# Moving small steps of a cached-attention decode kernel to GpSimd, one power for the inverse root, contiguous weights, and another order in the last batch

## The chip, the cores and the metric

The kernel runs on one core of one Trainium2 chip. The metric is the time of one execution on the device, in microseconds (us). The core has a matrix engine (PE, with its weight loads shown as PEld), a vector engine (DVE), a scalar engine (ACT), GpSimd (POOL), and a queue engine (SP) that issues the transfers; 16 transfer engines move data between HBM and the on-chip memories SBUF and PSUM. Each engine works through its own queue in order. Engines wait for one another through semaphores.

## The reference

Two layers, each an attention block with a key/value cache followed by a small MLP mixer, for 8 batch rows of one token each. Both layers use the same weights and the same caches. Cut to what matters:

```python
def attention(x, k_cache, v_cache, wq, wo):      # x: (8, 1, 448)
    q = (x @ wq).reshape(8, 1, 16, 256).transpose(0, 2, 1, 3)
    k = repeat(k_cache, 2, axis=1)               # k_cache: (8, 8, 4096, 256)
    v = repeat(v_cache, 2, axis=1)
    p = softmax(einsum("bhqd,bhkd->bhqk", q, k) * 256 ** -0.5)
    o = einsum("bhqk,bhkd->bhqd", p, v)
    return o.transpose(0, 2, 1, 3).reshape(8, 1, 4096) @ wo

def mixer(x, w1, w2, w3, w4):                    # one token: the shifted halves are zero
    x1 = x + hs                                  # hs is zero for S = 1
    return x1 + gelu(layernorm(x1) @ w3) @ w4    # w3: (448, 1792), w4: (1792, 448)

for layer in range(2):
    x = x + attention(layernorm(x), k_cache, v_cache, wq, wo)
    x = x + mixer(layernorm(x), w1, w2, w3, w4)
```

The caches are 8 x 8 x 4096 x 256 in bf16, 2 MB of K and 2 MB of V for each pair of batch row and KV head. All shifted channels of the one-token mixer come from outside the sequence, so hs is zero and w1 and w2 drop out of the computation.

## The kernel before

The work is cut into 128 jobs, called pairs: (layer, batch row, KV head). A pair loads K and V of its head, computes the scores of two query heads, a softmax, and the weighted sum of V, and adds its share of the output projection.

**Transfers and slots.** K and V go through 27 slots of 0.5 MB in SBUF. K of a pair is loaded in two runs of two slots each (lines 527 to 531), V in four single slots (544 to 549). All loads are issued on SP in one list: K of pair n comes ahead of V of pair n - 1 (lines 757 to 763). A load waits until its slot is free, that is, until PE has used the earlier content. The weights wq come first; wo, w3 and w4 follow the first pairs (384 to 392). For the heads in KEEP_HEADS (4 to 7), K of layer 0 stays in its 16 slots and layer 1 uses it again, so that those pairs of layer 1 load V only.

**Order of the pairs** (483 to 494). For each batch row b: layer 0 of b, then heads 0 to 3 of layer 1 of b - 1, then the kept heads 7 to 4 of layer 1 of b. At the very end come heads 0 to 3 of layer 1 of row 7, which load K and V.

**One pair** (from 509). DVE transposes K in SBUF (L536, eight per pair); PE computes scores into PSUM (L559); DVE takes the maximum of each partition (L566, pm) and spreads it over two columns, one for each query head (L568, pmh); GpSimd takes the maximum over all partitions (L570, gm); DVE picks the value that belongs to the partition's query head and multiplies by minus the scale (L572, nb); ACT computes the exponential with that bias and sums it (L576, p and rs); DVE transposes p (L581, pT) and spreads the sum over two columns (L583, rsh); GpSimd adds it over all partitions (L585, db); DVE takes the reciprocal (L587, rc). PE multiplies pT by V (L598); DVE transposes the result (L603, oX); four small matmuls put it together (L609); DVE scales it (L615, oT); PE adds its share of the output projection (L627, psM). Two sets of buffers alternate from pair to pair (par).

**After the last pair of a row** comes the tail (633): the residual (L645), two layer norms (norm_at, 702), w3 (L655), GELU (L662 to L674), w4 (L682), the residual again (L689, L690). In layer 0 a third norm, the query projection (L447) and expand (457) follow, which make layer 1's query; in layer 1 the row is written out (L697). A norm ends with an inverse square root: an initial guess from the bits of the number (L725, L726) and three Newton steps (L731 to L733), all on DVE.

**The planner.** Graph.schedule (145) is a list scheduler that runs while the program is built. It gives each task a start time from written durations and priorities (10 n for pair n, with small offsets), and the order that comes out is the fixed order of each engine's queue. Dependencies become semaphore waits. A list of operations given to Graph.add becomes a chain in which each step waits for the one before, on the same engine too (128 to 132).

**GpSimd's code.** Ahead of GpSimd's first affine_select (L352) the compiled program has an instruction that exchanges GpSimd's code, and ahead of its first partition_all_reduce (L570) a second one, which loads other code. They are in no line of the kernel.

Of the kernel before, what the change touches and what calls it, by code (L numbers as in the profile page):

```python
# [6 lines left out]
P = 128  # L7
B = 8
D = 448
HQ = 16  # L10
HKV = 8
SK = 4096
DH = 256
F = 1792
CP = 112
NCC = 4
# [8 lines left out]
RSQRT_MAGIC = 0x5F3759DF  # L25

NSLOT = 27
KEEP_HEADS = (4, 5, 6, 7)
TAIL_HEADS = (0, 1, 2, 3)
# [3 lines left out]
BIG = 3.0e38  # L33
# [28 lines left out]
class Res:  # L62


    def __init__(self, psum=False):
        self.prev = []
        self.writers = []
        self.readers = []
        self.psum = psum
# [10 lines left out]
    def write(self, t):  # L80
# [4 lines left out]
        for p in self.prev:  # L85
            t.deps.setdefault(p, False)
# [180 lines left out]
def bass_interleave_layers__gqa_block_cached__mixer_s_mlp__decode_kernel(  # L267
# [43 lines left out]
    rc = [sb(f"rc{i}", [P, 2], f32) for i in range(2)]  # L311
# [19 lines left out]

    kv_pool = Pool(NSLOT)
# [11 lines left out]
    def c_zero(e):  # L344
        e.memset(id4[:, :], 0.0)
        e.memset(qsel[:, :, :], 0.0)
        return e.memset(mneg[:, :], -1.0 / D)

    ops = [c_zero]
    for j in range(4):  # L350
# [11 lines left out]
        lambda e: e.tensor_scalar(cap[:, :], own[:, :], 2.0, -1.0, ALU.mult, ALU.add),  # L362
        lambda e: e.tensor_single_scalar(cap[:, :], cap[:, :], BIG, ALU.mult),
    ], 0.8, 0, reads=[res("const")], writes=[res("own")])

    def c_dve(e):
        e.memset(wo_sb[:, 32 * D:], 0.0)
# [4 lines left out]
        for i in range(4):  # L372
# [3 lines left out]
                                        res("wpad"), res("qx0"), res("qx1"), res("qx2"), res("qx3")])  # L376
# [8 lines left out]
    dma(lambda e: e.dma_start(wo_sb[:, 0:32 * D].rearrange("p (t n) -> p t n", n=D),  # L385
                              A_wo.rearrange("(t m) n -> m t n", m=P)),
# [3 lines left out]
    dma(lambda e: e.dma_start(w4_sb[:, 0:NFT * D].rearrange("p (t n) -> p t n", n=D),  # L390
                              B_w4.rearrange("(t m) n -> m t n", m=P)),
# [3 lines left out]
    def norm(tag, src, dst, bank, nb, prio, src_res, dst_res):  # L395
# [5 lines left out]
        st = sb(f"st_{tag}", [CP, 6, nb], f32)  # L401
        sti = sb(f"sti_{tag}", [CP, nb], i32)
        rL = res(f"ln_{tag}")

        def bc(ap):
# [13 lines left out]
        v, y, a = st[:, 0, :], st[:, 1, :], st[:, 2, :]  # L419
        ops = [  # L420
            lambda e: e.tensor_scalar(v, M[0:CP, 16:16 + nb], -1.0, LN_EPS, ALU.mult, ALU.add),
            lambda e: e.tensor_single_scalar(sti[:, :], v.bitcast(i32), 1, ALU.arith_shift_right),
            lambda e: e.tensor_scalar(sti[:, :], sti[:, :], -1, RSQRT_MAGIC, ALU.mult, ALU.add),
        ]
        y0 = sti[:, :].bitcast(f32)
        for it in range(3):
            yi = y0 if it == 0 else y
            ops.append(lambda e, yi=yi: e.tensor_tensor(a, yi, yi, ALU.mult))
            ops.append(lambda e: e.tensor_tensor(a, a, v, ALU.mult))
            ops.append(lambda e: e.tensor_scalar(a, a, -0.5, 1.5, ALU.mult, ALU.add))  # L430
            ops.append(lambda e, yi=yi: e.tensor_tensor(y, yi, a, ALU.mult))
        ops.append(lambda e: e.tensor_tensor(dst, xc[:, :, :], bc(y), ALU.mult))
        g.add("dve", ops, 0.18 * len(ops), prio, reads=[rM, rL], writes=[rL, dst_res])
# [23 lines left out]
    def expand(layer, b, prio):  # L457

        X = psX[1]
        rX = res("psX1", True)  # L460
# [6 lines left out]
        g.add("pe", f, 0.4, prio, reads=[res(f"q{b}"), res("const")], writes=[rX])  # L467
        for a in range(4):
# [5 lines left out]
            g.add("act" if a % 2 else "dve", cp, 0.3, prio, reads=[rX], writes=[res(f"qx{x}")])  # L474
# [7 lines left out]

    jobs = []
    for b in range(B):
        if b == 0:
            jobs += [(0, 0, h) for h in range(HKV)]
            jobs += [(0, 1, h) for h in TAIL_HEADS]
        else:
            done = TAIL_HEADS if b == 1 else ()
            jobs += [(0, b, h) for h in range(HKV) if h not in done]  # L490
            jobs += [(1, b - 1, h) for h in TAIL_HEADS]
# [408 lines left out]
```

## Time and profile before

| | |
|---|---|
| Median of 3 runs | 1246.17 us (1244.68 to 1247.53) |
| Profiled execution: its own time | 1247.13 us |
| Profiled execution: span | 1245.2 us, 41565 instructions |
| DVE busy | 806.7 us (65%), 2867 instructions |
| PE busy / PEld busy | 711.3 us (57%) / 514.7 us (41%) |
| ACT busy | 120.4 us (10%) |
| POOL busy | 99.8 us (8%), 271 instructions |
| Transfers | 483.03 MB, mean 388 GB/s |
| Mean granted PE clock | 0.62 |

The span runs from the first to the last instruction. A row of the timeline gives the start, the duration, the engine, the line, the operation, the tiles written and read with their shapes, and in brackets how long the engine had been idle and what it waited for; "issue" means that it waited for nothing that the profile shows. A row of windows gives the stretch, its length, the busy time of PE, PEld, DVE, ACT and POOL with the number of instructions, then the granted PE clock, the busy share of the transfer engines, and GB/s.

### The profile page before, as it was taken

The numbers are of one execution on the slowest core, as the hardware profiler recorded it, in microseconds if no ns is written. First come the engines' busy times: TensorE is split into PE (matmuls) and PEld (weight loads), VectorE is DVE, ScalarE is ACT, GpSimd is POOL, SyncE is SP. The second block draws the span as 40 slices with busy tenths as digits, with TensorE's granted clock in tenths as the row PEclk, the third lists the DMA queues.
The fourth block names the chain that finished last, engine by engine and source line by source line (L and its number), as shares of the span: only waits on it lengthen the run. The fifth ranks groups of instructions, "written<-read, shape, count | busy, mean of one in ns | idle before, by whom it ended". The sixth has DMA issues, their size and how long they took to land.

```text
span 1245.2 us, 41565 instructions
## 1 busy us (share of the span) xinstructions
PE 711.3 (57%) x18532; PEld 514.7 (41%) x18532; DVE 806.7 (65%) x2867; ACT 120.4 (10%) x305; POOL 99.8 (8%) x271
## 2 busy tenths in 40 slices
PE   2325566567545765457645676456754577545764
PEld 2212354355433643236523454235542365323653
DVE  5636747666767567675766667675676756767574
ACT  0100011001010111001100010100100011100110
POOL 0000001001000000000000000000100000000000
PEclk9999966556555665556655566555655556655665
DMA  9999999999999999999999999999999999999992
GB/s 303 405 351 414 406 378 414 413 407 369 402 414 408 365 412 408 412 403 373 404 414 404 398 378 394 413 412 404 367 407 414 402 360 414 402 414 407 363 395 92
DMA packets 109667, 483.03 MB, mean 388 GB/s; under 512 B 13264, under 2 KB 19152, under 8 KB 84688
## 3 DMA queue, kind: packets, MB, share of 16 engines
q1 hardware_dynamic: 108464, 480.37, 97.3%
q8 instruction: 145, 2.38, 0.8%
q14 instruction: 34, 0.28, 0.1%
q10 hardware_dynamic: 1024, 0.01, 0.0%
HBM read 480.32 MB, written 0.01 MB: 386 GB/s over the span
## 4 chain that ended last, share of the span: by engine, by line
DMA 56%; PE 23%; DVE 13%; issue 5%; SPq 2%; ACT 1%; POOL 0%; ACTq 0%
DMA kv<-in_A_v_cache_dram 39%; DMA kv<-in_A_k_cache_dram 15%; PE psO L598 8%; DVE kv L536 6%; PE psS L559 6%; PE psX L682 3%; PE psX L447 2%; DMA wo_sb<-in_A_wo_dram 2%; PE psM L627 2%; SPq L547 1%; DVE oX L603 1%; PE psX L655 1%; SPq L530 1%; DVE pT L581 1%; PE psX L713 1%
## 5 line engine op out<-in xcount | busy, mean ns | idle before, releaser
L536 DVE STREAM_TRANSPOSE kv<-kv 128x512 int32<-128x512 int32 x768 | 506.6, 691 | 84.9 <-DMA kv<-in_A_k_cache_dram 84.9
L598 PE MATMUL psO<-kv,pT 128*2 128x256 bf16 x4096 | 268.5, 393 | 153.5 <-DMA kv<-in_A_v_cache_dram 104.5
L559 PE MATMUL psS<-kv,qx 128*8 128x128 bf16 x8192 | 253.2, 294 | 144.2 <-DVE rc L587 65.3
L559 PEld LDWEIGHTS psS<-kv,qx 128*8 128x8 bf16 x8192 | 205.8, 117 | 173.7 <-DVE rc L587 67.1
L576 ACT ACTIVATE p<-psS,nb 128x256 bf16<-128x256 f32 x128 | 107.1, 836 | 910.1 <-DVE nb L572 867.0
L598 PEld LDWEIGHTS psO<-kv,pT 128*2 128x2 bf16 x4096 | 83.6, 94 | 256.5 <-DMA kv<-in_A_v_cache_dram 184.1
L627 PE MATMUL psM<-oT,wo_sb 128*128 128x1 bf16 x2048 | 87.0, 172 | 70.8 <-DVE oT L615 60.4
L566 DVE TENSOR_REDUCE pm<-psS 128x1 f32<-128x256 f32 x128 | 53.6, 418 | 107.3 <-PE psS L559 105.8
L603 DVE STREAM_TRANSPOSE oX<-psO 128x256 f32<-128x256 f32 x128 | 57.5, 449 | 85.8 <-PE psO L598 85.6
L627 PEld LDWEIGHTS psM<-oT,wo_sb 128*128 128x128 bf16 x2048 | 76.9, 117 | 84.7 <-DVE oT L615 68.2
L570 POOL PARTITION_ALL_REDUCE gm<-pmh x128 | 46.5, 363 | 748.4 <-DVE pmh L568 582.9
L585 POOL PARTITION_ALL_REDUCE db<-rsh x128 | 51.5, 402 | 362.9 <-DVE rsh L583 326.5
L609 PE MATMUL psO<-oX,id 128*32 128x4 f32 x1024 | 37.0, 200 | 50.4 <-DVE oX L603 22.9
L609 PEld LDWEIGHTS psO<-oX,id 128*32 128x32 f32 x1024 | 29.5, 141 | 80.4 <-DVE oX L603 45.2
L581 DVE STREAM_TRANSPOSE pT<-p 128x256 bf16<-128x256 bf16 x128 | 54.1, 423 | 5.1 <-ACT p L576 3.2
L682 PE MATMUL psX<-hT,w_sb 128*128 128x1 bf16 x896 | 32.5, 171 | 19.5 <-issue 11.9
L682 PEld LDWEIGHTS psX<-hT,w_sb 128*128 128x128 bf16 x896 | 30.9, 116 | 20.7 <-issue 12.3
L655 PE MATMUL psX<-n,w_sb 112*128 112x1 bf16 x896 | 26.1, 165 | 19.6 <-DVE n L734 19.6
L447 PE MATMUL psX<-n,wq_sb 112*128 112x1 bf16 x1024 | 29.0, 165 | 14.1 <-DVE n L734 13.1
L447 PEld LDWEIGHTS psX<-n,wq_sb 112*128 112x128 bf16 x1024 | 28.0, 104 | 14.2 <-DVE n L734 13.7
L576 ACT ACTIVATION_READ_ACCUMULATOR p<-psS,nb 128x1 f32 x128 | 33.6, 262 | 0.0
L655 PEld LDWEIGHTS psX<-n,w_sb 112*128 112x128 bf16 x896 | 25.0, 103 | 20.4 <-DVE n L734 20.4
(148 smaller groups left out, 380.6 us busy)
## 6 DMA issues: line engine op xcount, KB each, us to landing
kv<-in_A_v_cache_dram SPq DMA_DIRECT2D x512, 512.0 KB, 12.9
kv<-in_A_k_cache_dram SPq DMA_DIRECT2D x192, 1024.0 KB, 16.5
wq_sb<-in_A_wq_dram SPq DMA_DIRECT2D x1, 3584.0 KB, 17.5
wo_sb<-in_A_wo_dram SPq DMA_DIRECT2D x1, 3584.0 KB, 28.3
w_sb<-in_B_w_dram SPq DMA_DIRECT2D x2, 1568.0 KB, 25.8
out_dram<-xT ACTq DMA_DIRECT2D x8, 0.9 KB, 6.5
xT<-in_A_x_dram SPq DMA_DIRECT2D x1, 7.0 KB, 2.0
```

Of the source, the lines that this page charges most:

```text
L447: last = e.matmul(M[:, base + col * nb:base + (col + 1) * nb], wq_sb[:, k, f0:f0 + P], xn[:, :, k], start=(k == 0), stop=(k == NCC - 1))
L536: return e.transpose(ap, ap)
L559: last = e.matmul(S[32 * j:32 * j + 8, w * y:w * y + w], qx[x][:, h, 2 * c + u, :], kt[:, :, c, 8 * j:8 * j + 8, u], start=(c == 0 and u = ...
L566: g.add("dve", lambda e: e.tensor_reduce(pm[par][:, :], S[:, 0:256], axis=AX.X, op=ALU.max), 0.4, pr, reads=[rS], writes=[res(f"pm{par}")])
L576: g.add("act", lambda e: e.activation(p_sb[par][:, :].rearrange("p (z k y) -> p y z k", z=8, k=8), S[:, 0:256].rearrange("p (y z k) -> p y ...
L581: g.add("dve", lambda e: e.transpose(pT[par][:, :], p_sb[par][:, :]), 0.44, pr, reads=[rP], writes=[rPT])
L598: last = e.matmul(O[32 * j:32 * j + 2, 0:DH], pt[:, i, 2 * a:2 * a + 2], slot_ap(vin)[:, i * DH:(i + 1) * DH], start=(a == 0 and i < 4), s ...
L603: g.add("dve", lambda e: e.transpose(oX[par][:, :], O[:, 0:DH]), 0.4, pr, reads=[rO], writes=[res(f"oX{par}")])
L609: last = e.matmul(O[32 * a:32 * a + 32, 256:260], id4[:, :], oX[par][:, :].rearrange("p (c a r) -> p a c r", c=2, a=4)[:, a, :, 0:2], star ...
L627: last = e.matmul(psM[layer][:, c:c + 1], wo_sb[:, c0:c0 + 509:4], oT[:, jb, kt_:kt_ + 1], start=(first and k == 0 and c == 0), stop=False ...
L655: last = e.matmul(M[:, 32 + ft:33 + ft], w3_sb[:, c, ft * P:(ft + 1) * P], xa["n2"][:, 0, c:c + 1], start=(c == 0), stop=(c == NCC - 1))
L682: last = e.matmul(M[:, 64 + c:65 + c], w4_sb[:, c0:c0 + 509:4], hT[:, ft:ft + 1], start=(ft == 0), stop=(ft == NFT - 1))
```

## The change

- KEEP_HEADS and TAIL_HEADS become KEEP_RUNS, how many of a head's two K runs stay (2 for heads 4 to 7, as before). In the last row, layer 1's heads 0 to 3 come ahead of the kept heads.
- Every norm takes the inverse root as one operation on GpSimd, a power of -0.5 (against a tile pw filled with -0.5), between two DVE steps.
- pmh, nb and rsh move from DVE to GpSimd. nb, which was one DVE instruction with an accumulator, becomes a product and a sum. pmh adds a mask of 0 and -1e38 instead of taking a minimum.
- wo is loaded so that a partition holds four neighbouring rows of a head's 512, w4 so that a partition holds 14 neighbouring rows. oX, the four small matmuls and w3's columns are rearranged to fit. A partition then belongs to one query head, so rc has one column, made on GpSimd by a product with a mask (half) and a sum, and oT is a scaling by a per-partition scalar. rc's buffers order their writes against the reads on the same engine (strict).
- The four copies of expand are tracked one by one, so DVE's and ACT's no longer take turns.
- Some written durations of the planner differ.

```diff
-KEEP_HEADS = (4, 5, 6, 7)
-TAIL_HEADS = (0, 1, 2, 3)
+KEEP_RUNS = {4: 2, 5: 2, 6: 2, 7: 2}
-BIG = 3.0e38
+BIG = 1.0e38
...
         for p in self.prev:
+            if self.strict:
+                t.deps[p] = True
             t.deps.setdefault(p, False)
...
-        lambda e: e.tensor_scalar(cap[:, :], own[:, :], 2.0, -1.0, ALU.mult, ALU.add),
-        lambda e: e.tensor_single_scalar(cap[:, :], cap[:, :], BIG, ALU.mult),
+        lambda e: e.tensor_scalar(cap[:, :], own[:, :], -1.0, BIG, ALU.add, ALU.mult),
...
-    dma(lambda e: e.dma_start(wo_sb[:, 0:32 * D].rearrange("p (t n) -> p t n", n=D),
-                              A_wo.rearrange("(t m) n -> m t n", m=P)),
+    dma(lambda e: e.dma_start(wo_sb[:, 0:32 * D].rearrange("p (h f) -> p h f", h=HKV),
+                              A_wo.rearrange("(h m k) n -> m h (k n)", m=P, k=4)),
...
-    dma(lambda e: e.dma_start(w4_sb[:, 0:NFT * D].rearrange("p (t n) -> p t n", n=D),
-                              B_w4.rearrange("(t m) n -> m t n", m=P)),
+    dma(lambda e: e.dma_start(w4_sb[:, 0:NFT * D], B_w4.rearrange("(m t) n -> m (t n)", m=P)),
...
-        rX = res("psX1", True)
+        rX = [res(f"psX1_{a}", True) for a in range(4)]
...
         else:
-            done = TAIL_HEADS if b == 1 else ()
-            jobs += [(0, b, h) for h in range(HKV) if h not in done]
-            jobs += [(1, b - 1, h) for h in TAIL_HEADS]
-        jobs += [(1, b, h) for h in reversed(KEEP_HEADS)]
-    jobs += [(1, B - 1, h) for h in TAIL_HEADS]
+            jobs += [(0, b, h) for h in range(HKV) if b > 1 or h in KEEP_RUNS]
+            jobs += [(1, b - 1, h) for h in tail_heads]
+        if b == B - 1:
+            jobs += [(1, b, h) for h in tail_heads]
+        jobs += [(1, b, h) for h in keep_heads]
...
-        g.add("dve", lambda e: e.tensor_scalar(pm2[par][:, :], cap[:, :], pm[par][:, 0:1], None, ALU.min), 0.18, pr,
+        g.add("pool", lambda e: e.tensor_scalar(pm2[par][:, :], cap[:, :], pm[par][:, 0:1], None, ALU.add), 0.25, pr,
               reads=[res(f"pm{par}"), res("own")], writes=[res(f"pmh{par}")])
         g.add("pool", lambda e: e.partition_all_reduce(gm[par][:, :], pm2[par][:, :], P, ReduceOp.max), 0.45, pr,
               reads=[res(f"pmh{par}")], writes=[res(f"gm{par}")])
-        g.add("dve", lambda e: e.tensor_tensor_reduce(
-            out=nbx[par][:, :], in0=gm[par][:, :], in1=ownneg[:, :], scale=1.0, scalar=0.0,
-            op0=ALU.mult, op1=ALU.add, accum_out=nb_[par][:, 0:1]), 0.25, pr,
-            reads=[res(f"gm{par}"), res("own")], writes=[res(f"nb{par}")])
+        g.add("pool", [
+            lambda e: e.tensor_tensor(nbx[par][:, :], gm[par][:, :], ownneg[:, :], ALU.mult),
+            lambda e: e.tensor_tensor(nb_[par][:, :], nbx[par][:, 0:1], nbx[par][:, 1:2], ALU.add),
+        ], 0.5, pr, reads=[res(f"gm{par}"), res("own")], writes=[res(f"nb{par}")])
...
-        g.add("dve", lambda e: e.tensor_scalar(rs2[par][:, :], own[:, :], rs[par][:, 0:1], None, ALU.mult), 0.18, pr + 1,
+        g.add("pool", lambda e: e.tensor_scalar(rs2[par][:, :], own[:, :], rs[par][:, 0:1], None, ALU.mult), 0.25, pr + 1,
               reads=[res(f"rs{par}"), res("own")], writes=[res(f"rsh{par}")])
-        g.add("pool", lambda e: e.partition_all_reduce(db[par][:, :], rs2[par][:, :], P, ReduceOp.add), 0.5, pr,
+        g.add("pool", lambda e: e.partition_all_reduce(db[par][:, :], rs2[par][:, :], P, ReduceOp.add), 0.45, pr + 1,
               reads=[res(f"rsh{par}")], writes=[res(f"db{par}")])
-        g.add("dve", lambda e: e.reciprocal(rc[par][:, :], db[par][:, :]), 0.17, pr + 1,
-              reads=[res(f"db{par}")], writes=[res(f"rc{par}")])
+        g.add("pool", [
+            lambda e: e.tensor_tensor(dbx[par][:, :], db[par][:, :], half[:, :], ALU.mult),
+            lambda e: e.tensor_tensor(db1[par][:, :], dbx[par][:, 0:1], dbx[par][:, 1:2], ALU.add),
+        ], 0.5, pr + 1, reads=[res(f"db{par}"), res("half")], writes=[res(f"dh{par}")])
+        g.add("dve", lambda e: e.reciprocal(rc[par][:, :], db1[par][:, :]), 0.17, pr + 1,
+              reads=[res(f"dh{par}")], writes=[res(f"rc{par}")])
...
-        g.add("dve", lambda e: e.transpose(oX[par][:, :], O[:, 0:DH]), 0.4, pr,
+        g.add("dve", lambda e: e.transpose(oX[par][:, :].rearrange("p (c r) -> p c r", r=32),
+                                        O[:, 0:DH].rearrange("p (a r k) -> p a k r", a=2, k=4)), 0.4, pr,
...
-        g.add("dve", lambda e: e.tensor_tensor(
-            oT[:, jb, 4 * h:4 * h + 4].rearrange("p (j c) -> p c j", c=2),
-            O[:, 256:260].rearrange("p (c j) -> p c j", j=2),
-            rc[par][:, :].unsqueeze(1).to_broadcast([P, 2, 2]), ALU.mult), 0.2, pr,
+        g.add("dve", lambda e: e.tensor_scalar(
+            oT[:, jb, 4 * h:4 * h + 4], O[:, 256:260], rc[par][:, 0:1], None, ALU.mult), 0.2, pr,
...
-                    last = e.matmul(M[:, 32 + ft:33 + ft], w3_sb[:, c, ft * P:(ft + 1) * P], xa["n2"][:, 0, c:c + 1],
+                    last = e.matmul(M[:, 32 + ft:33 + ft], w3_sb[:, c, ft:ft + 127 * NFT + 1:NFT], xa["n2"][:, 0, c:c + 1],
...
-        for it in range(3):
-            yi = y0 if it == 0 else y
-            ops.append(lambda e, yi=yi: e.scalar_tensor_tensor(a, yi, v, yi, ALU.mult, ALU.mult))
-            ops.append(lambda e: e.tensor_scalar(a, a, -0.5, 1.5, ALU.mult, ALU.add))
-            ops.append(lambda e, yi=yi: e.tensor_tensor(y, yi, a, ALU.mult))
-        ops.append(lambda e: e.tensor_scalar(dst, xc[:, :, :], y, None, ALU.mult))
-        g.add("dve", ops, 0.18 * len(ops), prio, reads=[rM, rL], writes=[rL, dst_res])
+        v, y = st[:, 0:1], st[:, 1:2]
+        g.add("dve", lambda e: e.tensor_scalar(v, M[0:CP, 16:17], -1.0, LN_EPS, ALU.mult, ALU.add), 0.18, prio,
+              reads=[rM], writes=[rL])
+        g.add("pool", lambda e: e.tensor_tensor(y, v, pw[0:CP, 0:1], ALU.pow), 0.6, prio,
+              reads=[rL, res("const")], writes=[rL])
+        g.add("dve", lambda e: e.tensor_scalar(dst, xc[:, :, :], y, None, ALU.mult), 0.25, prio,
+              reads=[rL], writes=[rL, dst_res])
```

## The prediction

> **What bounds the kernel now.** I read the page's slices and shares first, then the windows, then the timelines of the end and of GpSimd (POOL). On the page, "DMA" is the busy share of the 16 transfer engines and "GB/s" what they moved:
>
> ```profile
> POOL 0000001001000000000000000000100000000000
> DMA  9999999999999999999999999999999999999992
> GB/s 303 405 351 414 406 378 414 413 407 369 402 414 408 365 412 408 412 403 373 404 414 404 398 378 394 413 412 404 367 407 414 402 360 414 402 414 407 363 395 92
> ```
>
> The transfers bound the kernel: at about 411 GB/s, 483.03 MB take 1175 us of the 1245.2. The rest is a slow start, a dip once per batch, and an end without transfers. POOL is idle 92% of the time. A dip, in windows (the last two columns are DMA share and GB/s), and what ends it:
>
> ```profile
> 1160.00:1165.00 5.00, 3.30 (x113) 3.22 (x114) 1.87 (x12) 0.00 (x0) 0.00 (x0) 0.50 1.03 409
> 1165.00:1170.00 5.00, 3.71 (x101) 3.35 (x102) 2.48 (x14) 0.52 (x2) 0.00 (x0) 0.50 0.74 293
> 1170.00:1175.00 5.00, 4.19 (x150) 3.35 (x138) 3.03 (x19) 0.84 (x2) 1.11 (x3) 0.68 0.75 240
> ...
> 1168.57 3.37 PE L559 MATMUL psS<-kv,qx 128*8 128x128 bf16 x119 [0.17 <-ACT qx L473]
> ```
>
> Layer 1's scores wait for its query, so slots stay full. The dip costs 5 x (116 + 169)/409 = 3.5 us; the same sum over the eight dips (from 175, 280, 425, 575, 720, 870, 1020 and 1165 us) gives 25.4 us.
>
> One pair's small steps, unloaded, at the end of the run (columns: start, duration):
>
> ```profile
> 1219.38 0.42 DVE L566 TENSOR_REDUCE pm<-psS 128x1 f32<-128x256 f32 x1 [0.40 <-PE psO L609]
> ...
> 1219.84 0.23 DVE L568 TENSOR_SCALAR pmh<-cap,pm 128x2 f32<-128x2 f32 x1
> ...
> 1220.16 0.36 POOL L570 PARTITION_ALL_REDUCE gm<-pmh  x1 [3.10 <-DVE pmh L568]
> 1220.55 0.16 DVE L572 CUSTOM_DVE_ANT_0 nbx<-gm,ownneg 128x2 f32<-128x2 f32 x1 [0.48 <-POOL gm L570]
> 1220.64 0.08 DVE L572 DVE_READ_ACCUMULATOR2_ANT nb<- 128x1 f32 x1
> 1220.82 0.83 ACT L576 ACTIVATE p<-psS,nb 128x256 bf16<-128x256 f32 x1 [4.96 <-DVE nb L572]
> ```
>
> Finally POOL's first instructions. Each row ends with its idle time before and the releaser:
>
> ```profile
> 1.24 0.19 POOL L347 MEMSET mneg<- 112x112 f32 x1
> 11.99 0.32 POOL L352 TENSOR_SCALAR_AFFINE_SELECT qsel<-qsel 128x128 bf16<-128x128 bf16 x1 [10.56 <-issue]
> ...
> 14.14 0.21 POOL L355 TENSOR_SCALAR_AFFINE_SELECT id<-id 128x32 f32<-128x32 f32 x1
> 32.96 0.38 POOL L570 PARTITION_ALL_REDUCE gm<-pmh  x1 [18.61 <-DVE pmh L568]
> ```
>
> This is what decides my forecast. POOL stands 10.56 us ahead of its first AFFINE_SELECT and waits for nothing that the profile shows. In the compiled program an instruction that exchanges GpSimd's code stands there, and a second, for other code, stands ahead of the first PARTITION_ALL_REDUCE, where 18.61 us of idle time would hide it. MEMSET ran before either. So one set of code serves AFFINE_SELECT and another the all-reduce, and an exchange costs up to 10.56 us. Before pays for two, because after the constants POOL runs only all-reduces (256).
>
> **The change, part by part.**
>
> *Small steps to POOL.* Per pair this takes pmh (203 ns), nbx with its accumulator read (141 + 83) and rsh (196) off DVE: 26.0 + 18.1 + 10.7 + 25.0 = 79.8 us of DVE's 806.7, beside the transfers. It puts on POOL one TENSOR_SCALAR and two TENSOR_TENSOR around each of the two all-reduces. No POOL row shows these. One costs between 0.10 (MEMSET 128x1) and 0.40 us (all-reduce); I take 0.21, the 128x32 AFFINE_SELECT, the nearest in kind. POOL's chain for a pair, without exchanges: six steps x 0.21 = 1.26, all-reduces 0.36 + 0.40, the exponential in between 0.1 + 0.82 + 0.1 (1220.82 to 1221.64 with its accumulator read), and six waits on its own results x 0.1 (the all-reduce starts 0.09 after pmh ends) = 0.6: together 3.6 us.
>
> Whose code do the new steps need? If they are resident as MEMSET is, no exchange. If they share the all-reduce's code, one at the start. If they need AFFINE_SELECT's or other code, the order "scale, all-reduce, multiply, add; scale, all-reduce, multiply, add" changes code four times per pair, in a queue that runs in order. I take four: the profile's own name for the instruction that asked for the first set is TENSOR_SCALAR_AFFINE_SELECT, so the tensor-scalar family is the nearest row, and it is not in the all-reduce's set.
>
> Price of an exchange, from rows: above, 10.56 us, seen while the transfer engines were 0.85 to 1.06 busy; below, 1.28 us, ScalarE's ACT_TABLE_LOAD, the only other load of this kind that shows. With the transfer engines idle I take midway, 5.92; beside the stream, 10.56. In a run of some 4200 us the stream needs 1175, a share of 0.28: 0.28 x 10.56 + 0.72 x 5.92 = 7.22 us. A pair then holds POOL for 4 x 7.22 + 3.6 = 32.5 us, against 9.5 us of transfers. 128 x 32.5 = 4160 us. Nothing overlaps it: each exchange lies between two steps of one chain, and the next pair's steps queue behind it on POOL; the exponential waits for them, then pT, PV, the slots and SP's transfers.
>
> The Trainium skill, GPSIMD Engine Reference, section Instruction dispatch, says that GpSimd's kernels are loadable code and that the first call after a load pays about 6 us (5.95 measured), with no instruction visible in the profile. Put in for the 7.22, that gives 128 x (4 x 5.95 + 3.6) + 82 = 3590 us, an estimate. Its section Engine selection speaks against the change outright: elementwise work belongs on VectorE.
>
> *Inverse root.* In the end's norm the chain runs from 1228.05 to DVE's last step at 1230.53: 2.48 us. It becomes one DVE step (0.17), a hop (0.09), the power and a hop back (0.03). The power lies between 0.10 and 0.40 us by POOL's rows; at 0.40, the dearer, it saves 1.8 us. Two norms lie on the end's path: 3.6. The other 38 and the prologue's go beside POOL's chain. A power needs no exchange where it falls among the other new steps. In layer 0's tail, the Newton steps queue between K transposes (0.69 us each) for 7.9, 8.1 and 2.7 us (1126.59 to 1134.53, 1138.62 to 1146.69, 1159.37 to 1162.11). Without them the query comes some 15 us sooner, which would close the dips if transfers still set the pace. POOL may wait for powers and queries: 0 to 48 us over 16 tails (3 each); I take 30.
>
> *wo and w4.* The page's "under 2 KB" minus "under 512 B" is 5888 pieces, which is 4096 + 1792 of 896 B: exactly wo and w4. They become 1024 pieces of 3584 B and 128 of 12.5 KB. Between 52 and 76 us the stream lost 5.4 us. V's 4 KB pieces run at 411 GB/s, so 0 to 5.4 is gained; I take 4.8, hidden when POOL sets the pace. w3's weights are then read at a stride of 14: between L655's 1.66 and L682's (stride 4) 1.97 us for 56 matmuls, so 0 to 0.3 us per tail.
>
> *Order of the last batch.* K's transposes (about 5.2 us per pair) leave the last four pairs; oX came every 8.8 and 7.0 us there, a V-only pair needs 5.1 us of transfers. With the hole at 1207 to 1209 (1.4) this is 0 to 3.2 us, hidden in the POOL case, too. On SP's queue 8 K and 16 V transfers move ahead of 16 V transfers; kept K then holds 16 of the 27 slots for four pairs more. Batch 6's four pairs ran like that at 385 to 421 GB/s (1120 to 1140 us), so that costs at most 5 x (411 - 385)/411 = 0.3 us in a window.
>
> *The rest.* Two copies of the query run side by side (about 0.8 us per expansion); oX, the four small matmuls, oT and rc keep their sizes (within 0.05 us each); the four memsets of half lie in DVE's idle 4.3 to 14.4. The new planner durations reorder the queues; no row prices that, and I allow 10 us either way (a third of what dips and weights lose together).
>
> *Sum* against the profiled execution (1247.13 = span 1245.2 + 1.9; 0.96 above the median of 1246.17): start to the first all-reduce 33.0, pairs 4160, waits 30, end 20.1 (1225.06 to 1245.2) - 3.6 = 16.5: span 4240, **4240 us** with the 1.9.
>
> **Rivals.**
> - *No exchanges (faster).* The steps are resident as MEMSET is: POOL needs 3.6 us per pair, far below 9.5. Then three quarters of the dips (19; PE, at 3.3 to 4.2 of 5 us there, keeps some) go, with 4.8 of the weights and about 5 of the end: 1247 - 29 = 1218 us. For it: MEMSET ran freely. Against: AFFINE_SELECT didn't. It also decides if exchanges are cheap: 4 x s + 3.6 stays below 9.5 while s is under 1.5 us, as at the lower row's 1.28.
> - *Two exchanges per pair.* If half of the changes fall away (neighbouring all-reduces, or one kind shared): 128 x (2 x 7.22 + 3.6) + 82 = 2390 us. The fixed chain of a pair speaks against it.
> - *Exchanges always at full price*, if loading doesn't get faster without the stream: 128 x (4 x 10.56 + 3.6) + 82 = 5950 us. It is the forecast's upper end; at 5.92 each the forecast is 3574.
>
> **How the numbers follow.** Four exchanges per pair: 0.86, with 0.06 of it near full price. Two: 0.03. None or cheap: 0.11, of which 0.01 lands within 0.2%, about what a measurement of this kernel can tell from no change. So faster 0.10, same 0.01, slower 0.89. The range leaves out the rivals on the near side and a little more, and goes from 3300 (an exchange of 5.4 us) to 6000.
>
> **What would show it.** Right: POOL rows with idle times of 5 to 11 us "<-issue" ahead of each all-reduce and of the step after it, some 500 of them; DMA share near 0.3; the chain of waits mostly issue or POOL. Wrong: a POOL TENSOR_TENSOR within 0.3 us of its all-reduce; then the dips, the 52 to 76 us stretch and the Newton rows tell how much of the 29 us came.

## The result, and the profile after

The changed kernel takes 4695.7 us (median of 4 runs, 4679.3 to 4711.3) where the kernel before takes 1245.4 us beside it: 3.770 times as long, with a 95% interval of 3.756 to 3.784. The profiled execution took 4711.25 us, with a span of 4709.3.

The slices of the page after, where the transfers stood at 411 GB/s before, and the shares of the chain that ended last:

```profile
DMA  8113412332123321233212332123321233213230
GB/s 295 72 72 121 152 50 112 125 112 87 66 112 125 112 84 68 112 125 112 81 72 111 126 112 81 68 113 127 112 81 69 113 128 112 82 62 116 108 116 1
issue 81%; DVE 7%; POOL 6%; PE 3%; ACT 2%; POOLq 1%; DMA 0%; ACTq 0%; SPq 0%
```

The transfers are no longer the bound. 81% of the chain is "issue", time in which an engine waits for nothing that the profile shows. GpSimd's waits (engine, line and what ended the wait; then us in total, times, longest) say where:

```profile
POOL gm L574 <- issue: 1035.9, 128, 11.5
POOL dbx L592 <- issue: 941.9, 121, 12.2
POOL nbx L577 <- issue: 844.6, 114, 12.0
POOL db L589 <- issue: 809.9, 127, 9.0
POOL pmh L572 <- DVE pm L570: 420.4, 104, 22.7
POOL rsh L587 <- ACT p L580: 131.8, 126, 1.3
```

Ahead of each all-reduce (gm, db) and of the first step behind it (nbx, dbx) stands a wait of 6 to 8 us on average: four per pair. In the compiled program 511 instructions exchange GpSimd's code, for 2 before. The trace fits them: behind the first AFFINE_SELECT, GpSimd's queue goes 510 times from an all-reduce to an elementwise step or back, and each of these 510 steps has waited for "issue", 5.7 us or more. The fifth row is a different wait, for the next pair's maximum (its longest, 22.65 us, stands ahead of the very first pair, which leaves 398 us between the pairs). One pair and the start of the next, in the timeline of the kernel after (start, duration; in brackets the idle time before, and the releaser):

```profile
2054.99 0.41 POOL L589 PARTITION_ALL_REDUCE db<-rsh  x1 [6.64 <-issue]
2063.00 0.19 POOL L592 TENSOR_TENSOR dbx<-db,half 128x2 f32<-128x2 f32 x1 [7.60 <-issue]
2063.26 0.19 POOL L593 TENSOR_TENSOR db<-dbx 128x1 f32<-128x1 f32 x1
2063.49 0.16 DVE L595 RECIPROCAL rc<-db 128x1 f32<-128x1 f32 x1 [14.64 <-POOL db L593]
...
2065.43 1.07 PE L563 MATMUL psS<-kv,qx 128*8 128x128 bf16 x32
...
2067.48 0.42 DVE L570 TENSOR_REDUCE pm<-psS 128x1 f32<-128x256 f32 x1 [0.62 <-PE psS L563]
...
2068.02 0.31 POOL L572 TENSOR_SCALAR pmh<-cap,pm 128x2 f32<-128x2 f32 x1 [4.56 <-DVE pm L570]
...
2079.30 0.37 POOL L574 PARTITION_ALL_REDUCE gm<-pmh  x1 [10.98 <-issue]
```

Two steps of the same kind follow each other at once (dbx, then db at 2063.26); a change of kind costs 6.64, 7.60 and 10.98 us here. The row of 2063.49 shows the second loss: DVE, which works in order, has stood for 14.64 us at the reciprocal of the old pair, and only behind it come the work that lets PE make the next pair's scores (here the copies of layer 1's query, in most pairs the transposes of K, for which PE waits 1720.2 us in all), and their maximum. GpSimd, which has just got its elementwise code back, waits 4.56 us more for that maximum.

A pair takes (4689.5 - 31.2)/128 = 36.4 us, from the first pair's first step on GpSimd to the last pair's last. The sum of the four "issue" rows, with the smaller ones of the same kind (51.8 ahead of db's second step, 58.4 and 43.6 ahead of 14 powers), is 3786 us: 29.6 per pair, 7.40 each.

### The profile page after: what moved, and what is told of

It is laid out like the page before. It is cut to its first block, busy times and chain, and to the rows that moved or that the text cites. A ratio compares the mean times of both kernels' runs of the same rounds, so it can differ in the third digit from the quotient of the medians.

```text
span 4709.3 us, 42358 instructions
## 1 busy us (share of the span) xinstructions
PE 754.1 (16%) x18532; PEld 557.9 (12%) x18532; DVE 729.1 (15%) x1904; ACT 119.5 (3%) x305; POOL 300.5 (6%) x1081
## 4 chain that ended last, share of the span: by engine, by line
issue 81%; DVE 7%; POOL 6%; PE 3%; ACT 2%; POOLq 1%; DMA 0%; ACTq 0%; SPq 0%
DVE kv L540 5%; ACT p L580 2%; PE psS L563 2%; POOL db L589 1%; POOL gm L574 1%; DVE pm L570 1%; POOL rsh L587 1%; POOL pmh L572 1%; POOL nb L578 1%; POOL db L593 1%; POOL dbx L592 1%; POOL nbx L577 1%; DMA kv<-in_A_k_cache_dram 0%; DVE rc L595 0%; POOLq L592 0%
## 5 line engine op out<-in xcount | busy, mean ns | idle before, releaser
L563 PE MATMUL psS<-kv,qx 128*8 128x128 bf16 x8192 | 257.5, 301 | 2220.8 <-DVE kv L540 1720.2
L540 DVE STREAM_TRANSPOSE kv<-kv 128x512 int32<-128x512 int32 x768 | 492.3, 681 | 20.6 <-DMA kv<-in_A_k_cache_dram 20.5
L563 PEld LDWEIGHTS psS<-kv,qx 128*8 128x8 bf16 x8192 | 192.2, 115 | 2280.8 <-DVE kv L540 1764.0
L595 DVE RECIPROCAL rc<-db 128x1 f32<-128x1 f32 x128 | 21.0, 164 | 1818.3 <-POOL db L593 1818.3
L606 PEld LDWEIGHTS psO<-kv,pT 128*2 128x2 bf16 x4096 | 116.5, 115 | 578.2 <-issue 541.0
L662 PE MATMUL psX<-n,w_sb 112*128 112x1 bf16 x896 | 56.4, 198 | 226.3 <-DVE n L733 226.3
L592 POOL TENSOR_TENSOR dbx<-db,half 128x2 f32<-128x2 f32 x128 | 23.6, 185 | 941.9 <-issue 941.9
L662 PEld LDWEIGHTS psX<-n,w_sb 112*128 112x128 bf16 x896 | 55.1, 160 | 230.1 <-DVE n L733 230.1
L577 POOL TENSOR_TENSOR nbx<-gm,ownneg 128x2 f32<-128x2 f32 x128 | 23.6, 184 | 844.6 <-issue 844.6
L572 POOL TENSOR_SCALAR pmh<-cap,pm 128x2 f32<-128x2 f32 x128 | 38.9, 304 | 422.8 <-DVE pm L570 420.4
L587 POOL TENSOR_SCALAR rsh<-own,rs 128x2 f32<-128x2 f32 x128 | 38.8, 303 | 131.8 <-ACT p L580 131.8
```

The lines of the kernel that those rows point to most:

```text
L540: return e.transpose(ap, ap)
L563: last = e.matmul(S[32 * j:32 * j + 8, w * y:w * y + w], qx[x][:, h, 2 * c + u, :], kt[:, :, c, 8 * j:8 * j + 8, u], start=(c == 0 and u = ...
L572: g.add("pool", lambda e: e.tensor_scalar(pm2[par][:, :], cap[:, :], pm[par][:, 0:1], None, ALU.add), 0.25, pr, reads=[res(f"pm{par}"), re ...
L577: lambda e: e.tensor_tensor(nbx[par][:, :], gm[par][:, :], ownneg[:, :], ALU.mult),
L587: g.add("pool", lambda e: e.tensor_scalar(rs2[par][:, :], own[:, :], rs[par][:, 0:1], None, ALU.mult), 0.25, pr + 1, reads=[res(f"rs{par}" ...
L606: last = e.matmul(O[32 * j:32 * j + 2, 0:DH], pt[:, i, 2 * a:2 * a + 2], slot_ap(vin)[:, i * DH:(i + 1) * DH], start=(a == 0 and i < 4), s ...
```

## Experiments

Two theories were set against each other first. Theory 1: GpSimd exchanges its code whenever its queue changes between an all-reduce and an elementwise step. Theory 2: the price hangs on the moved small steps themselves, and not on what they alternate with. Later runs ask where the sum went wrong, and what the other parts of the change are worth.

| Run | What it is | Time (us) | Ratio to before, 95% | Exchanges in the program |
|---|---|---|---|---|
| after | the whole change | 4695.7 | 3.756 to 3.784 | 511 |
| e1 | after, small steps and Newton on DVE | 1258.3 | 1.0126 to 1.0176 | 2 |
| e2 | after, all-reduces replaced | 1226.3 | 0.9855 to 0.9902 | 1 |
| e3 | e1 with rsh alone on GpSimd | 2767.5 | 2.222 to 2.236 | 258 |
| e4 | after, small steps on DVE | 1381.3 | 1.1103 to 1.1152 | 51 |
| e5 | after, planner's durations corrected | 4156.1 | 3.333 to 3.354 | 509 |
| e6 | before, small steps on GpSimd | 4090.7 | 3.280 to 3.302 | 510 |
| e7 | e1 with the order of before | 1247.3 | 1.0006 to 1.0044 | 2 |
| e8 | e7 with w3 and w4 as before | 1241.6 | 0.9974 to 1.0011 | 2 |
| e9 | after, dbx and db on DVE | 4047.2 | 3.250 to 3.273 | 501 |
| e10 | e8, inverse root on ScalarE | 1225.1 | 0.9852 to 0.9891 | 2 |
| e11 | e8, two Newton iterations | 1229.0 | 0.9882 to 0.9929 | 2 |
| e12 | e10 and e11 together | 1223.9 | 0.9848 to 0.9887 | 2 |

### Is it the change of code?

**e4: the small steps back on DVE, the powers left on GpSimd.**

```diff
-        g.add("pool", lambda e: e.tensor_scalar(pm2[par][:, :], cap[:, :], pm[par][:, 0:1], None, ALU.add), 0.25, pr,
+        g.add("dve", lambda e: e.tensor_scalar(pm2[par][:, :], cap[:, :], pm[par][:, 0:1], None, ALU.add), 0.18, pr,
```

(likewise nbx and nb, rsh, dbx and db)

> As e1, but the inverse root is the power on POOL: 51 exchanges, those around the powers of the 16 tails. Theory 1 (alternation): each exchange runs beside the full stream and takes 8 to 11.5 us, as the dearest of the changed kernel did; two of them ahead of a pair's all-reduce are more than the 13 us that 11 free slots buffer, so about half a tail's 18 us or more is lost in most of the 16 tails: 1290 to 1400 us. Theory 2 (the steps themselves): 41 powers of 0.6 us, hidden, and the shorter norms close the dips: 1200 to 1225 us.

1381.3 us, as theory 1 had it and 156 us above the upper end of theory 2. The waits of e4's GpSimd for "issue" name the cause, a power between two all-reduces:

```profile
POOL gm L574 <- issue: 119.5, 15, 11.4
POOL st_0c L731 <- issue: 86.3, 8, 11.9
POOL st_1a L731 <- issue: 84.5, 8, 12.3
POOL st_0a L731 <- issue: 77.7, 8, 11.6
```

Against e1, which differs in the power alone, that is 123 us: the inverse root as one power is itself a loss of 10% while the all-reduces stand on the same engine. An exchange costs 9.7 to 10.8 us ahead of these powers (86.3/8, 84.5/8, 77.7/8), beside a stream above 380 GB/s in most of them, and 8.0 back (119.5/15).

**e2: no all-reduce at all.** Each of the two becomes an elementwise GpSimd instruction that copies the partition's own value, so the maximum and the sum over the partitions are left out.

```diff
-e.partition_all_reduce(gm[par][:, :], pm2[par][:, :], P, ReduceOp.max)
+e.tensor_scalar(gm[par][:, :], pm2[par][:, :], one1[:, 0:1], None, ALU.mult)
-e.partition_all_reduce(db[par][:, :], rs2[par][:, :], P, ReduceOp.add)
+e.tensor_scalar(db[par][:, :], rs2[par][:, :], one1[:, 0:1], None, ALU.add)
```

> The changed kernel with both all-reduces replaced by one more elementwise TENSOR_SCALAR on POOL each, so that POOL never changes its code after the start. It leaves out the maximum and the sum over the partitions; everything else, all the new POOL steps and the power among them, stays. Theory 1 (alternation): 1200 to 1235 us, POOL rows follow one another without idle time of several us that nothing explains. Theory 2 (the steps themselves): above 4000 us, since POOL has two steps more of the new kind. Theory 3 (order, layout, planner): near 4700.

1226.3 us with all eight elementwise steps of a pair on GpSimd. The steps follow one another at once; the longer waits are for other engines:

```profile
607.25 0.29 POOL L574 TENSOR_SCALAR pmh<-cap,pm 128x2 f32<-128x2 f32 x1 [5.05 <-DVE pm L572]
607.63 0.29 POOL L576 TENSOR_SCALAR gm<-pmh,one 128x2 f32<-128x2 f32 x1
608.01 0.19 POOL L579 TENSOR_TENSOR nbx<-gm,ownneg 128x2 f32<-128x2 f32 x1
```

Theory 2 falls: the same steps cost nothing where nothing alternates with them.

**e3: one step of the pair on GpSimd** (rsh), Newton and the other steps on DVE, so that neighbouring all-reduces of two pairs have nothing between them.

```diff
 # e1, and:
-        g.add("dve", lambda e: e.tensor_scalar(rs2[par][:, :], own[:, :], rs[par][:, 0:1], None, ALU.mult), 0.18, pr + 1,
+        g.add("pool", lambda e: e.tensor_scalar(rs2[par][:, :], own[:, :], rs[par][:, 0:1], None, ALU.mult), 0.25, pr + 1,
```

> As e1, but of the six small steps one, rsh (the spreading of the sums, TENSOR_SCALAR 128x2), stays on POOL between the two all-reduces: 258 exchanges in the compiled program instead of 511 or 2. Theory 1 (alternation): two exchanges of about 7.4 us per pair, of which the first overlaps the exponential (1.3 us), plus some 3 us of chain: 16 to 19 us per pair, 2050 to 2500 us; idle time of 5 to 11 us ahead of rsh and ahead of the second all-reduce, and none ahead of the first. Theory 2 (each new step costs its share): a sixth of the loss of 3450 us, about 1820 us.

Two exchanges per pair, as theory 1 says, but 2767 us, above its range. A pair of e3 in the timeline:

```profile
1399.75 0.29 POOL L597 TENSOR_SCALAR rsh<-own,rs 128x2 f32<-128x2 f32 x1 [9.34 <-issue]
1405.92 0.41 POOL L599 PARTITION_ALL_REDUCE db<-rsh  x1 [5.88 <-issue]
...
1411.21 0.37 POOL L584 PARTITION_ALL_REDUCE gm<-pmh  x1 [4.88 <-DVE pmh L582]
...
1419.95 0.29 POOL L597 TENSOR_SCALAR rsh<-own,rs 128x2 f32<-128x2 f32 x1 [8.37 <-issue]
```

The exchanges took 8.8 (1126.5/128) and 6.8 us (823.7/121), 15.6 of a pair's 21.2 ((2745.9 - 33.5)/128, from the first all-reduce to the last). Nearly 5 us more pass between the two all-reduces in these rows, for the next pair's K transposes, scores and maximum on DVE and PE, which stand behind the denominator. My range had no term for that; it is the same gap as in the forecast.

**e6: the small steps alone, on the kernel before.**

```diff
 # before, and only:
-        g.add("dve", lambda e: e.tensor_scalar(pm2[par][:, :], cap[:, :], pm[par][:, 0:1], None, ALU.min), 0.18, pr,
+        g.add("pool", lambda e: e.tensor_scalar(pm2[par][:, :], cap[:, :], pm[par][:, 0:1], None, ALU.add), 0.25, pr,
```

(likewise nbx and nb, and rsh; pmh's mask changes with it; the denominator has no sum in this layout)

> The kernel before with the small steps of a pair alone moved to GpSimd: 510 exchanges; norms, weights, order and durations otherwise as before. If the small steps alone are the cause: 510 exchanges of 7.4 us (3774 us), 300 us of GpSimd's own work and a wait of the kind seen ahead of pmh, so 4400 to 4800 us, within 5% of the changed kernel. If another part of the change were needed for the slow-down (the power between the steps, the new order): under 3000 us.

4090.7 us: the small steps alone make 2845 us of the slow-down, but the 4400 to 4800 was missed from below. 510 exchanges, one fewer than after, and 605 us less time: the changed kernel loses something else, too.

### What the other 605 us are

**e9: the denominator's product and sum back on DVE**, as one instruction that reads the all-reduce.

```diff
-        g.add("pool", [
-            lambda e: e.tensor_tensor(dbx[par][:, :], db[par][:, :], half[:, :], ALU.mult),
-            lambda e: e.tensor_tensor(db1[par][:, :], dbx[par][:, 0:1], dbx[par][:, 1:2], ALU.add),
-        ], 0.5, pr + 1, reads=[res(f"db{par}"), res("half")], writes=[res(f"dh{par}")])
+        g.add("dve", lambda e: e.tensor_tensor_reduce(
+            out=dbx[par][:, :], in0=db[par][:, :], in1=half[:, :], scale=1.0, scalar=0.0,
+            op0=ALU.mult, op1=ALU.add, accum_out=db1[par][:, 0:1]), 0.25, pr + 1,
+            reads=[res(f"db{par}"), res("half")], writes=[res(f"dh{par}")])
```

> The changed kernel with one of its steps undone: the denominator's product and sum (dbx, db) are again one DVE instruction that reads the all-reduce's result; 501 exchanges stay. Theory A (what the changed kernel takes over e6's 4091 us comes from that step alone: on GpSimd it stands behind an exchange, DVE's reciprocal waits for it, and the next pair's maximum stands behind the reciprocal, so one of the four exchanges and the next pair's preparation come one after the other): the reciprocal follows the all-reduce directly, the exchange back runs beside the next pair's preparation, the pmh wait for DVE's pm falls from 420 to under 120 us: 4050 to 4200 us. Theory B (the new order, the powers on GpSimd or the durations make the difference): 4550 to 4720 us.

4047.2 us, theory A and 3 us beyond its range. Ten exchanges fewer explain 74 us; the span fell by 664. The same place in e9's timeline:

```profile
2080.10 0.41 POOL L589 PARTITION_ALL_REDUCE db<-rsh  x1 [6.00 <-issue]
2080.54 0.16 DVE L591 CUSTOM_DVE_ANT_0 dbx<-db,half 128x2 f32<-128x2 f32 x1 [6.37 <-POOL db L589]
...
2084.90 0.42 DVE L570 TENSOR_REDUCE pm<-psS 128x1 f32<-128x256 f32 x1 [1.13 <-PE psS L563]
...
2087.21 0.29 POOL L572 TENSOR_SCALAR pmh<-cap,pm 128x2 f32<-128x2 f32 x1 [6.70 <-DVE kv L540]
```

DVE goes on 0.03 us after the all-reduce, and the next pair's maximum is done at 2085.32, while the exchange back is still running (to 2087.21). In the kernel after, DVE went on only after that exchange, so the two came one behind the other. Most of it can be read in the waits: exchanges and pmh's waits together are 3786 + 420 = 4206 after, and here 857.7 (gm) + 817.3 (db) + 907.2 (nbx) + 861 (pmh, whatever ended it) + 183 (powers) = 3626, 580 of the 664; the two steps that left GpSimd, 0.45 us a pair (2063.00 to 2063.45 above), are 58 more. (pmh's wait has a new name here, since the last semaphore to come was DVE's, but the exchange is inside it.)

**e5: only the planner's durations corrected.**

```diff
-e.partition_all_reduce(gm[par][:, :], pm2[par][:, :], P, ReduceOp.max), 0.45, pr,
+e.partition_all_reduce(gm[par][:, :], pm2[par][:, :], P, ReduceOp.max), 7.8, pr,
```

(likewise the other all-reduce; 8.2 for the two steps behind each)

> The changed kernel with only the planner's durations corrected: 7.8 us for an all-reduce and 8.2 us for the two steps behind it, which is what they cost with their exchanges in the profile after. It still has 509 exchanges. Theory A (the 420.4 us for which GpSimd waits ahead of pmh come from DVE's queue, which was laid out for steps of 0.45 us and so stands at the reciprocal while the next pair's scores and maximum are behind it): the planner now puts the next pair's work ahead of that reciprocal, the wait falls to under 100 us, and the time to 4300 to 4400 us. Theory B (the wait lies in the chain of one pair itself, whatever the order): the wait stays near 420 us and the time within 50 us of 4696.

4156.1 us: theory A, and more than it asked for. Of the waits for DVE's maximum one is left, 22.4 us ahead of the first pair, and gm's exchange is cheaper, 746.3/126 = 5.9 us where it was 8.1:

```profile
POOL db L589 <- issue: 826.3, 127, 8.6
POOL gm L574 <- issue: 746.3, 126, 7.9
POOL rsh L587 <- issue: 638.3, 64, 12.8
POOL pmh L572 <- issue: 506.0, 58, 14.8
```

Others are dearer in return, 638.3/64 = 10.0 us ahead of rsh and 506.0/58 = 8.7 ahead of pmh, so that all of e5's exchanges together take 3631 us, 155 less than after. The rest of the gain is the wait for the maximum.

The price of an exchange goes with the stream beside it. Three windows, of after, e5 and e9, each the time of one exchange ahead of gm (last two columns: DMA share and GB/s):

```profile
2068.00:2079.30 11.30, 1.89 (x74) 1.49 (x72) 1.15 (x6) 0.00 (x0) 0.31 (x1) 0.62 1.01 398
```

```profile
2033.40:2039.30 5.90, 4.25 (x120) 3.48 (x120) 1.32 (x3) 0.83 (x2) 0.00 (x0) 0.55 0.01 4
```

```profile
2087.60:2096.80 9.20, 0.00 (x0) 0.00 (x0) 0.61 (x2) 0.00 (x0) 0.00 (x0) 0.50 0.62 257
```

10.98 us at 398 GB/s, 5.94 at 4, 9.30 at 257. Over all 255 exchanges to the all-reduce's code in the kernel after, the 74 with under 20 GB/s beside them took 5.99 us on average, and the 15 with over 380 took 10.0, but single ones from 6.4 to 11.5: the rate alone doesn't fix the price. In after the pair's new transfers go out just when gm's exchange begins; in e5's window it runs with the stream at rest.

### What the other parts are worth

**e1: all of the change but the steps and the power** (pieces as in e4, and before's Newton steps).

> The changed kernel with the six small steps of a pair and the inverse root (Newton steps) back on DVE; contiguous weights, the new order of the last batch, the split copies and the planner durations stay. POOL then runs only the all-reduces after the constants, so the compiled program exchanges GpSimd's code twice instead of 511 times. Theory 1 (the alternation between the all-reduce's code and the elementwise code costs the time): 1205 to 1240 us, about 5 us from the weights and up to 5 at the end below the 1245 of before. Theory 2 (the new steps themselves are slow on POOL): the same, 1205 to 1240. Theory 3 (the new order, the new layout or the planner durations cost the time): far above 1300.

1258.3 us: not faster but 1.3 to 1.8% slower than before. Something else in the change costs more than it brings. e1's windows show a hole at the new order of the last batch:

```profile
1160.00:1165.00 5.00, 0.68 (x16) 0.59 (x16) 4.64 (x19) 0.00 (x0) 0.00 (x0) 0.50 0.98 399
1165.00:1170.00 5.00, 3.51 (x128) 3.49 (x128) 1.44 (x6) 0.00 (x0) 0.00 (x0) 0.50 0.07 29
1170.00:1175.00 5.00, 4.01 (x119) 3.81 (x120) 3.50 (x20) 0.52 (x2) 0.06 (x1) 0.50 0.19 23
```

Before ran at 293 and 240 GB/s in the last two. SP's queue stands for 14.3 us for layer 1's scores, which wait for their query (the longest such wait of before in this stretch: 10.3).

**e7: e1 with before's order of the last batch.**

```diff
-        if b == B - 1:
-            jobs += [(1, b, h) for h in tail_heads]
         jobs += [(1, b, h) for h in keep_heads]
+    jobs += [(1, B - 1, h) for h in tail_heads]
```

> e1 (all of the change but the steps and the power on GpSimd) with the last batch in the order of before. e1 took 1258.3 us, 13 to 16 more than before. If the new order is why: its stream stood at 29 and 23 GB/s from 1165 to 1175 us, which is 5 x (382 + 388)/411 = 9.4 us lost, where before lost 3.5 there; 5.9 us come back: 1250 to 1254. If the order is innocent: 1256 to 1261, and the cause is the weights read at a stride or the planner's durations.

1247.3 us: 11.0 less than e1 (nearer 16 by the two ratios to before, 1.0151 and 1.0025), twice or more what the hole at 1165 us explained. A second one of e1, at 1200 to 1210 us (215 and 342 GB/s), would be worth 5 x (196 + 69)/411 = 3.2 us; 2 us, or 7 by the ratios, stay open. The new order is a loss.

**e8: w3 and w4 as before, too.**

```diff
-w3_sb[:, c, ft:ft + 127 * NFT + 1:NFT]
+w3_sb[:, c, ft * P:(ft + 1) * P]
```

(and w4's load as before, in pieces of 896 B)

> e7 with w3 and w4 laid out as before too (w3's weight loads contiguous, w4 in pieces of 896 B), so that wo alone is contiguous. If the stride of 14 costs what the changed kernel's end shows (3.52 for 1.66 us, 1.9 per tail, one of them on the end's path and the others ahead of a query): 2 to 6 us under e7, so 1246 to 1251 by the order theory. If the small pieces of w4 cost more than the stride: above e7 by up to 2 us.

1241.6 us, under the range and 5.7 below e7 (their intervals just overlap). The weight loads of w3 in e7's layout, shown by e1, and in e8's (mean ns of one ahead of the bar that gives the idle time):

```profile
L672 PEld LDWEIGHTS psX<-n,w_sb 112*128 112x128 bf16 x896 | 55.3, 160 | 30.5 <-DVE n L751 25.0 <-issue 2.3 <-DVE kv L550 1.9
```

```profile
L672 PEld LDWEIGHTS psX<-n,w_sb 112*128 112x128 bf16 x896 | 25.2, 104 | 32.4 <-DVE n L751 24.5 <-issue 4.3 <-DVE pT L595 2.0
```

A column stride of 14 makes a weight load 160 ns for 104, so each tail's 56 take 3.5 us for 1.7. What is left of the change in e8 (contiguous wo, the copies side by side, the layout of oX, other planner durations) can't be told from no change.

**e10: the inverse root on ScalarE.** e8, with every tail norm but the last tail's as a logarithm and an exponential.

```diff
+        g.add("act", lambda e: e.activation(v, M[0:CP, 16:17], ACT.Ln, bias=eps1[0:CP, 0:1], scale=-1.0), 1.5, prio,
+              reads=[rM, res("const")], writes=[rL])
+        g.add("act", lambda e: e.activation(y, v, ACT.Exp, scale=-0.5), 1.5, prio, reads=[rL], writes=[rL])
+        g.add("dve", lambda e: e.tensor_scalar(dst, xc[:, :, :], y, None, ALU.mult), 0.25, prio,
+              reads=[rL], writes=[rL, dst_res])
```

> e8 with the inverse root of all tail norms but the last tail's as two ScalarE steps, a logarithm and an exponential, in place of the eleven DVE steps. 76 table loads of about 1.28 us (97 us) come with it, on an engine that is 10% busy. If DVE's queue is what makes the dips (the Newton steps between K transposes): the query of layer 1 comes 5 to 8 us sooner and the dips go as in e2, which lost 29.9 us of transfers up to 1205 us for 44.4 of before: 12 to 16 us under e8, 1225 to 1231. If the norm's hops are not on the dips' path: 1238 to 1244. If the loads hold up the exponentials of the pairs: above e8.

1225.1 us, 1.1 to 1.5% faster than before: the norm's hops were on the path of the dips. The price is 76 table loads, and ScalarE, with time to spare, bears it. One norm of e10's layer 0:

```profile
1107.73 1.28 ACT L757 ACT_TABLE_LOAD   x1 [2.53 <-DVE rc L607]
1109.74 0.26 ACT L757 ACTIVATE st_0a<-psX,eps 112x1 f32<-112x1 f32 x1 [0.72 <-PE psX L739]
1110.01 1.28 ACT L759 ACT_TABLE_LOAD   x1
1111.31 0.20 ACT L759 ACTIVATE st_0a<-st_0a 112x1 f32<-112x1 f32 x1
...
1111.54 0.23 DVE L760 TENSOR_SCALAR n<-xc_0a,st_0a 112x4 bf16<-112x4 f32 x1 [0.84 <-ACT st_0a L759]
```

From the variance to n it is 1.8 us, where the prediction showed 7.9 for the same norm among the K transposes (6.6 in e8); the first load runs before the variance is there. Transfers lost between 80 and 1190 us, counted over all windows of 5 us that ran under 411 GB/s, fall from 32.2 us in e8 to 19.0.

**e11: two Newton iterations for three, in e8.**

```diff
-        for it in range(3):
+        for it in range(2):
```

> e8 with two Newton iterations for three in every norm (three or four DVE steps fewer per norm). If the chain of small DVE steps sets the dips and the end: at the end twice 3 steps of 0.17 us, 1.0 us; in the dips three steps of eleven with the transposes between them, a quarter to a third of what e10 may bring, 3 to 5 us: 1236 to 1238. If not: within 1 us of e8.

1229.0 us, under the range: against before e11 is at 0.9906 and e8 at 0.9992, so it brings 0.86%, 10.7 us, where 3 to 5 were expected. The dips' loss falls to 24.0 us. I had priced the steps alone; with what stands between them, layer 0's three norms shorten from 6.6, 6.8 and 3.7 us to 4.9, 5.6 and 2.1.

**e12: both.** e10 with two iterations in the norms that still have them.

> e10 with two Newton iterations in the two norms that still have them, the last tail's, and in the prologue's. If only the end's path is left to gain from it: twice 3 steps of 0.17 us at the end and 4 steps at the start, 1 to 2 us under e10: 1222 to 1225, ratio 0.984 to 0.987. If the gains of e10 and e11 over e8 added up as different work: 12 us or more under e10, near 1215.

1223.9 us, at 0.9848 to 0.9887 of before, the fastest here though not separable from e10. The gains of e10 and e11 don't add up: they are the same dips, whose loss is 19.9 us here and 19.0 in e10. The 1 us expected at the end is too small to be told from noise.

## Why the prediction was right, and where its sum was off

*Direction and mechanism: right.* Elementwise steps need other code than the all-reduce; four exchanges per pair, nothing overlaps them, the transfers stop being the bound. The inference from one idle row ahead of an AFFINE_SELECT held. e2 and e4 show it: without alternation no price, with 49 further exchanges than e1 10% more time.

*An exchange at 7.22 us: right within 3%* (7.40; 3786 us in all, 89 more than the sum's 512 x 7.22 = 3697). The mix of an idle price and a price beside the stream was right in kind: 5.6 to 6 us to the all-reduce and about 7 back at rest, against the 5.92 taken, and mostly 9 to 11 beside the full stream. That the 5.92 came so near was luck: it was the middle between 10.56 and the 1.28 of another engine's load. The Trainium skill's page GPSIMD Engine Reference (Instruction dispatch) states 5.95 us for the first call after a load; the rows agree with it for the all-reduce with the stream at rest, and nowhere else: its sum of 3590 us was too low by 1119.

*3.6 us of own steps per pair: right.* 36.4 - 29.6 (exchanges) - 3.1 (pmh's waits between the pairs, 400/128) leaves 3.7, with the powers and the waits for them in it. Its parts were off both ways: TENSOR_TENSOR took 0.19 us and TENSOR_SCALAR 0.30 for the 0.21 taken.

*"POOL may wait for powers and queries", 30 us: the step that failed.* The powers it names made 33 us of waits (17.6 + 7.4 + 5.8 + 2.4). But the sum had the next pair's maximum ready whenever GpSimd asked for it, queries apart. GpSimd waited 420.4 us for it, 398 of them between the pairs, 3.1 us per pair. I took DVE, freed of four steps and idle most of the time, to be ahead; I didn't ask what stood at the head of its queue. It was the reciprocal, DVE's longest wait in all, on its line of the page after:

```profile
L595 DVE RECIPROCAL rc<-db 128x1 f32<-128x1 f32 x128 | 21.0, 164 | 1818.3 <-POOL db L593 1818.3
```

e9 removes that order and 664 us of span. The span passed 4240 by 469 us: 368 from this term (398 for 30), 89 from the exchanges, and 12 from smaller ones of either sign.

*Inverse root.* At the end it saved 1.61 us per norm (0.87 for 2.48), 1.8 predicted: the power takes 0.55 to 0.59 us, above the 0.40 that I had as its dear end. "A power needs no exchange where it falls among the other new steps" held: 14 powers wait for one (the 58.4 and 43.6 us above), but each stands just ahead of a step of the pair (nbx or dbx), which then waits for none.

*w3 at a stride of 14: 0 to 0.3 us per tail was wrong.* The end's 56 matmuls took 3.52 us for 1.66. I took the stride of 4 as the nearest row, and a stride of 14 costs far more. With the power's smaller saving that makes the end 18.8 us for 16.5.

*wo and w4: 4.8 us was wrong, too.* The pieces of 896 B are gone, as predicted, and the slow stretch stays. Between 50 and 80 us before lost 5.3 us, e8, with wo contiguous, 4.4, and e7, with both contiguous, 4.6: a gain of less than 1 us. From 65 to 70 us e8 runs at 228 GB/s, with 213 before. What slows it stays open.

*Order of the last batch: 0 to 3.2 us gained, or 0.3 lost, was wrong in sign.* e7 against e1 gives a loss of 11 us or more. Both were hidden in the changed kernel.

*The rivals.* The one without exchanges stood at 1218 us; e2, which makes its condition true, took 1226. Its dips shrank (25.0 us lost between 80 and 1190 us, for 39.0 before); the losses by the order (11 us) and by w3 (5.7 with w4), which this rival's sum lacked, are large enough for the 8 us, but no run takes them out of e2. "Two exchanges per pair", 2390 us, came up 377 too low in e3, for want of the same term as the forecast.

## What to carry to other kernels

Before moving a step to another engine, look at what that engine runs on either side of it: a cheap instruction between two of another kind can cost the engine a load of code each time, which shows in a profile only as idle time that waits for "issue". When a result gets slower by a known amount, follow it to the in-order queue that reads it and price everything that stands behind that reader, here the whole next pair. Where a chain of tiny steps is slow because other work is queued between its links, shortening it, or giving it to an idle engine that needs no change of code with each step of the main loop, brought about 1% here (e11 and e10 against e8).

## Unexpected in the hardware

- *GpSimd's code seems to stay from one execution to the next.* The first AFFINE_SELECT of the kernel before waits 10.56 us, as the prediction showed. After:

```profile
1.97 0.32 POOL L360 TENSOR_SCALAR_AFFINE_SELECT qsel<-qsel 128x128 bf16<-128x128 bf16 x1 [0.50 <-POOL mneg L355]
```

  All kernels here whose last GpSimd instruction is an all-reduce (before, e1, e3, e6, e7, e8, e10, e11, e12) wait 9.9 to 10.8 us there; all that end with an elementwise one (after, e2, e4, e5, e9) wait 0.24 to 0.50. That the code of the execution before is still there is the reading that fits all of them, but it is not shown: no run was made for it alone.
- *An exchange can take almost twice as long beside a full stream*: 5.94 us at 4 GB/s, 10.98 at 398.
- *A weight load at a column stride of 14 takes 160 ns*, 104 where it is contiguous.
